# Attention and mixer on one core: the fourth batch's q loaded in token order and turned by DMA transposes

## The chip, the cores and the metric

The kernel runs on one core of one Trainium2 chip. The time is that of the device in microseconds (us), from a whole execution; smaller is better. The profile comes from one execution that the hardware profiler recorded. Its engines are PE (matrix products), PEld (the loading of PE's weights, beside PE), DVE (vector work), ACT (activations), POOL (here mostly the issue of loads that also convert from f32 to f16) and SP (here the issue of stores and of DMA transposes). DMA transfers themselves run on 16 DMA engines.

## What is computed

Attention over a batch of 8, with 8 heads, 576 tokens and 64 columns to a head. Each head has 16 extra keys and values ("beacons") that every token sees; among the 576 tokens the mask is causal. Its output x, 576 tokens by 512 columns to a batch, goes into a mixer: a product of rank 32 along the tokens, then a network of two products with a width of 2048, with both inputs added back.

```python
k_all = np.concatenate([beacon_k, k], axis=2)
v_all = np.concatenate([beacon_v, v], axis=2)
scores = scale * np.matmul(q, k_all.transpose(0, 1, 3, 2))
scores = np.where(causal, -1000000000.0, scores)
a = softmax(scores)                      # written out in the reference
x = np.matmul(a, v_all)                  # heads side by side: (8, 576, 512)
...
h = x.transpose(0, 2, 1) @ U @ V
u = x + h.transpose(0, 2, 1)
out = u + np.maximum(u @ w_ch1, 0.0) @ w_ch2
```

## The kernel before, in words

**Batches and pairs.** The 8 batches are b = 0 to 7; the first is b = 0, so the fourth batch is b = 3. A batch has four pairs of heads, p = 4b to 4b + 3; c = p mod 4 is the pair's place in its batch. The scores of a pair need q and k "turned": 128 rows of head columns (two heads of 64) by tokens. The tiles are qT (one to a batch, two buffers in rotation, for all four pairs) and kTs (two fixed tiles, by b mod 2).

**Two ways to turn.** Up to the fourth batch (b < `DT0` = 4) q and k are loaded by `token_load` so that a partition holds six tokens in a row of each head: 1536 bytes in a piece in memory, 768 bytes once in f16, one load to four heads (`HALVES`). For each pair `regroup` (L290, L292) lets DVE copy the two heads side by side into the tile pr, six identity products on PE turn it (tps, `in_pair`, L297), and one DVE copy moves the 576 columns from PSUM into qT or kT and puts the tokens in order (`qkT_units`, L330; a small one for the beacons of k, L335). From the fifth batch on, `load_whole` loads q and k "whole": five parts of up to 128 tokens, one token to a partition, all eight heads beside one another (L852; a piece is one head of one token, 64 columns, 128 bytes in f16). `turns` then issues five DMA transposes each for q and k from SP (L869); each turns one part for all four pairs.

**Staging.** q and k of a batch land in the tiles st1 and st0, with two buffers each (`qk_tiles`). The buffer of an earlier batch can be loaded again once all its readers are done: regroupings, or DMA transposes.

**Order.** All engines work through instructions in the order in which the program writes them. The loop over pairs p = 8 to 31 does so for the part that matters here. At p = 8 (b = 2, c = 0) `load_batch(3)` issues the loads of the fourth batch on POOL's queue: beacons of k, then k and q by halves of the heads, then v in five parts. At p = 10 `load_whole(4)` appends the loads of the fifth batch, which are issued one with each unit of mixer work. At p = 12 `load_batch(4)` issues v of the fifth batch, `turns(4)` is begun (its first five transposes on SP), then the five transposes uT<-xb of the mixer for b = 2 (`mix_units`, L455), then the other five of `turns(4)`. At p = 13 the loads of b = 5 follow, at p = 15 its transposes.

For p = 8 to 11 the lines in `third` give the order by words: `r` regroups a pair, `q` and `k` turn and evict it, `v` issues scores of pairs and column groups, `m` masks, `a` and `b` are the products with v of the two heads, `f` takes one unit from the queue of mixer work. So "r11 q10 f k10 m8 f v9:123 ..." is p = 8. From p = 12 on `long_slot` gives the order; there the q and k units of pairs 14 and 15 come from the list qk.

**Mixer work between.** The mixer's units are a queue: for each block of 512 rows 16 units g (gps) and then units of the second product (cps in blocks 0 and 1, mps later). Block 0's four stores of ob (L796) and block 1's four transposes ut<-uT (L745), which bring the mixer's input back to rows for the final sum (L790), are issued on SP while pairs 8 to 10 run. For each batch from b = 2 on the five uT<-xb transposes put x into uT, and DVE then adds the rank 32 product to uT in place (`settle`, L476); the next mixer blocks read it.

Of the kernel before, what the change touches and what calls it, by code (L numbers as in the profile page):

```python
# [30 lines left out]
def kernel(  # L31
# [13 lines left out]
    nc = tc.nc  # L45
# [13 lines left out]
    nk = [min(P, SK - P * c) for c in range(NC)]  # L59

    q0 = [max(0, P * j - Nb) for j in range(NC)]
    nq = [min(S, P * (j + 1) - Nb) - q0[j] for j in range(NC)]
    NT = NC
# [42 lines left out]
    def pst(shape, dtype, name):  # L106

        b = emptied.pop(0)
        t = psum.tile(shape, dtype, tag=f"bank{b}", name=name)
        bank_of[id(t)] = (b, t)  # L110
        return t

    def emptying(t):
        emptied.append(bank_of.pop(id(t))[0])
# [62 lines left out]
    kTs = [const.tile([P, NH2, NC * P], F16, name=f"kT{i}", tag=f"kT{i}") for i in range(2)]  # L177
    vss = [const.tile([P, NC * H * E], F16, name=f"vs{i}", tag=f"vs{i}") for i in range(2)]
# [41 lines left out]
    def beacon_load(eng, src, dst, hs):  # L220
        eng.dma_start(out=dst[0:Nb], in_=src[hs].rearrange("h p d -> p h d"))

    def token_load(eng, src, dst, hs):
        eng.dma_start(out=dst[0:TP, hs, :], in_=src[hs].rearrange("h (p j) d -> p h (j d)", j=TJ))  # L224

    def key_beacons(eng, src, dst, hs):
        beacon_load(eng, src, dst[TP:TB, hs, (TJ - 1) * D : TJ * D], hs)
# [4 lines left out]
    def v_beacon(bsrc, vs):  # L232
        beacon_load(nc.gpsimd, bsrc, by_head(vs)[:, 0, :, 0:D], ALLH)

    def v_tokens(src, vs, hs, js=range(NT)):
        dst = by_head(vs)[:, :, hs, 0:D]
        for j in js:
            a = Nb if j == 0 else 0
            nc.gpsimd.dma_start(  # L239
                out=dst[a : a + nq[j], j, :, :], in_=src[hs, ds(q0[j], nq[j]), :].rearrange("h p d -> p h d")  # L240
            )

    def v_loads(src, bsrc, vs):
        v_beacon(bsrc, vs)
        v_tokens(src, vs, ALLH)

    def by_token(t):
        return t.rearrange("p h (j d) -> p j h d", j=TJ)

    ALLH = slice(0, H)  # L250

    def qk_tiles():

        t = [stage.tile([P, TJ * DM], F16, name=f"st{i}", tag=f"st{i}") for i in range(2)]
        st = [x[:, :].rearrange("p (h e) -> p h e", h=H) for x in t]
        whole = [x[:, 0 : NT * DM].rearrange("p (j h d) -> p j h d", h=H, d=D) for x in t]
        return st, whole

    def emit_loads(b, L, vs):
        key_beacons(nc.gpsimd, beacon_k[b], L[0][0], ALLH)  # L260
        for hs in HALVES:
            token_load(nc.gpsimd, k[b], L[0][0], hs)
            token_load(nc.gpsimd, q[b], L[0][1], hs)
        v_loads(v[b], beacon_v[b], vs)


    def keep_warm(ps, n, a=ident):
# [15 lines left out]
    def regroup(st, c, i, *copies, beacons=True):  # L283

        t = pairs.tile([P, TJ, 2, D], F16, name=f"pr{i}", tag=f"pr{i}")
        src = by_token(st[i][:, 2 * c : 2 * c + 2, :])
        w = TJ // len(copies)
        for a, copy in enumerate(copies):
            js = slice(w * a, w * (a + 1))
            copy(out=t[0:TP, js], in_=src[0:TP, js])  # L290
        if i == 0 and beacons:
            copies[0](out=t[TP:TB, TJ - 1], in_=src[TP:TB, TJ - 1])  # L292
        return t
# [15 lines left out]
    def beacons_apart(st, kT, c, copy):  # L309

        ps = pst([P, Nb], F16, name="tpb")
        for h in range(2):
            nc.tensor.transpose(
                ps[ds(D * h, D), :], st[TP:TB, 2 * c + h, ds(D * (TJ - 1), D)], ident[TP:TB, TP:TB]
            )
        copy(out=kT[:, c, 0:Nb], in_=ps)
        emptying(ps)

    def qkT_units(turns, qT, kT, c, copies=((nc.vector.tensor_copy,), (nc.vector.tensor_copy,)), apart=None):

        def one(i, dst, b0):
            w = TJ // len(copies[i])
            bs = 0 if apart else b0
            whole = dst[:, c, b0 : b0 + S].rearrange("x (p j) -> x p j", j=TJ)
            for a, copy in enumerate(copies[i]):
                ps = pst([P, TP * w + bs], F16, name="tps")
                for j in range(w * a, w * a + w):
                    n = TP + bs if j == TJ - 1 else TP
                    turns[i](ps, TP * (j - w * a), n, j)
                copy(  # L330
                    out=whole[:, :, ds(w * a, w)],
                    in_=ps[:, 0 : TP * w].rearrange("x (j p) -> x p j", j=w),
                )
                if bs and a == len(copies[i]) - 1:
                    copies[i][0](out=dst[:, c, 0:b0], in_=ps[:, TP * w : TP * w + b0])  # L335
                emptying(ps)
            if b0 and apart:
                beacons_apart(apart, dst, c, copies[i][0])

        return [lambda: one(1, qT, 0), lambda: one(0, kT, Nb)]  # L340
# [492 lines left out]
    Ls, qTs, xbs = {}, {}, {}  # L833
    coming = []

    def load_batch(b):
        if b < DT0:
            Ls[b] = qk_tiles()
            emit_loads(b, Ls[b], vss[b % 2])
        else:  # L840
            coming.append(lambda: v_beacon(beacon_v[b], vss[b % 2]))
            coming.extend(lambda j=j: v_tokens(v[b], vss[b % 2], ALLH, [j]) for j in range(NT))
# [15 lines left out]
        while coming:  # L858
            coming.pop(0)()

    def turns(b):

        all_coming()
        new_qT(b)
        kn, qn = Ls[b][1]
        k_of = lambda j: (kn, kTs[b % 2], P * j, nk[j], j)
        q_of = lambda j: (qn, qTs[b], q0[j], nq[j], j)
        return [
            lambda n=n, dst=dst, o=o, m=m, j=j: nc.sync.dma_start_transpose(  # L869
                out=dst[:, :, ds(o, m)], in_=n[:m, j, :, :].rearrange("p h d -> p (h d)")  # L870
            )
            for n, dst, o, m, j in [k_of(0), *map(q_of, range(NT)), *map(k_of, range(1, NT))]
        ]

    HALVES = [slice(0, H // 2), slice(H // 2, H)]
# [19 lines left out]
    prs = {}  # L895
    V = nc.vector.tensor_copy

    def regroup_of(p):
        b, c = divmod(p, NH2)
        prs[p] = [regroup(Ls[b][0], c, i, nc.vector.tensor_copy) for i in range(2)]  # L900

    for i in range(2):
        nc.vector.memset(kTs[i][:, :, SK : NC * P], 0.0)
# [15 lines left out]
    def qkT_of(p):  # L919
        b, c = divmod(p, NH2)  # L920
        new_qT_of(p)
        copies = [(act_copy, nc.vector.tensor_copy) if p == 0 else (nc.vector.tensor_copy,)] * 2
        turns = by_heads(Ls[b][0], c)
        for i, t in enumerate(prs.get(p, ())):
            if t is not None:
                turns[i] = in_pair(prs[p])[i]
        return qkT_units(turns, qTs[b], kTs[b % 2], c, copies, Ls[0][0][0] if p == 0 else None)

    def expts_of(p):
        return [(lent if p in (2, 3) else expts)[(2 * p + i) % NE] for i in range(2)]  # L930
# [8 lines left out]
    def av_of(p):  # L939
        b, c = divmod(p, NH2)  # L940
        if c == 0:
            assert not coming or b < DT0
            xbs[b] = xbp.tile([P, NT, DM], F16, name="xb", tag="xb")
# [8 lines left out]
    ON_PE = (0, 1, 4)  # L952

    DT0 = 4
    LAG = 10
    HINT = 5
    FAST = 2
# [10 lines left out]
    def fill_turns(tr, n):  # L968
        for u in tr[:n]:
            u()  # L970
        del tr[:n]
# [25 lines left out]
    def mix(b):  # L997
# [3 lines left out]
        if turned:  # L1001
            turn()
        n = 0 if not turned else LAG + 3 if b == B - 1 else min(LAG, len(queue) - 8)
        k = 2 if turned else 1
# [31 lines left out]
    with tc.manual_schedule(engines={ENG.PE, ENG.Activation, ENG.DVE, ENG.SP, ENG.Pool}):  # L1036
# [15 lines left out]
        for u in qkT_of(1):  # L1052
            u()
# [48 lines left out]
        part = state["part"]  # L1102
# [41 lines left out]

        P6 = (DT0 - 1) * NH2
        mixing = []
# [22 lines left out]
        def long_slot(p, c, av, qk):  # L1169

            if c == 0:
                go([(p + 1, 0), (p + 1, 1), (p + 1, 2)], 1)
                fill(1)
                weighted(av[0:1] + qk[0:1] + av[1:2] + qk[1:2], 1, 1, 0, 1)
                if p + 3 < DT0 * NH2:
                    regroup_of(p + 3)
# [42 lines left out]
        for p in range(NP1, NP):  # L1219
            b, c = divmod(p, NH2)  # L1220
            if c == (1 if b >= DT0 else 0) and b + 1 < B:
                load_batch(b + 1)
            if c == (1 if b + 1 == DT0 else 2) and DT0 <= b + 2 < B:
                load_whole(b + 2)
            qk = qkT_of(p + 2) if P6 <= p and p + 2 < min(NP, DT0 * NH2) else []
            if c == 0 and DT0 <= b + 1 < B and b != DT0:
                tr = turns(b + 1)
            if c == NH2 - 1 and b + 1 == DT0:
                tr = turns(b + 2)
            if c in (0, NH2 - 1) and b + 1 == DT0:  # L1230
                fill_turns(tr, NT)
            if p == P6:
                mix_between(b - 1)
            if c == 0 and b + 1 >= DT0:
                fill_turns(tr, 2 * NT)
            if p < P6:
                play(third[c])
            else:
                long_slot(p, c, av_of(p), qk or [lambda: None] * 2)
# [60 lines left out]
    with tc.If(n_bad != 0, label="general"):  # L1300
        with tc.For_i(0, B, 1) as bi:
            L = qk_tiles()
# [13 lines left out]
            for t0 in range(0, S, 512):  # L1316
                n = min(512, S - t0)
# [32 lines left out]
```

## Time and profile before

| | us |
|---|---|
| median of three timed runs | 343.14 |
| lowest and highest of them | 341.88, 347.04 |
| the profiled execution | 340.93 |
| its span, first to last instruction | 339.3 |
| PE busy in the span | 329.8 |
| DVE busy | 234.1 |
| ACT busy | 178.7 |
| POOL busy | 136.1 |

The granted clock of PE was 1.00 throughout. Rows of a timeline read: start in us from the span's start, duration, engine, line of the kernel, operation, out<-in, shapes and count, and in brackets the idle time before with what ended it; the first start of a row that joins several instructions, and the whole stretch, are given. "SPq" is SP's queue, whose rows are the issue of a DMA, not its transfer. Rows of the DMA view read: what is moved, which queue, how many in the window asked for, KB of each, and last the median time from issue to landing in us. A landing is the point from which a reader may start.

### The profile page before, as it was taken

What the parts mean: (1) busy time and instruction counts of PE and PEld (TensorE: products, weight loads), DVE (VectorE), ACT (ScalarE), POOL (GpSimd) and SP (SyncE); (2) the same over time, 40 slices, a digit from 0 to 9 for tenths busy, and PEclk for the clock granted to TensorE, in tenths of its full rate; (3) what the DMA queues carried; (4) which work ended last, traced back from release to release, by engine and by line L of the source; (5) the groups of instructions that cost most, each with busy time, mean ns of one, the idle gap of its engine ahead of it and who ended that gap; (6) DMA issues with size and microseconds to landing.
All of it is one profiled execution on the core that took longest, in us unless ns stands there. A gap on an engine that the chain in (4) does not pass through costs nothing.

```text
span 339.3 us, 8838 instructions
## 1 busy us (share of the span) xinstructions
PE 329.8 (97%) x3494; PEld 212.0 (62%) x3494; DVE 234.1 (69%) x585; ACT 178.7 (53%) x383; POOL 136.1 (40%) x175
## 2 busy tenths in 40 slices
PE   8799999999999999999999999999999999999993
PEld 4465655455555456865688888755875675585493
DVE  6586885689989748765876677687776963743652
ACT  5957951478851677257734784468445403502500
POOL 8986724765140900677066805040130014013041
PEclk9999999999999999999999999999999999999999
DMA  8999999999997994999999999944213304104113
GB/s 159 141 175 138 183 196 194 200 192 139 138 118 152 153 141 86 101 169 157 151 112 155 187 143 104 132 140 87 66 64 93 73 31 126 31 33 124 31 37 99
DMA packets 150832, 41.97 MB, mean 124 GB/s; under 512 B 132096, under 2 KB 149696, under 8 KB 150784
## 3 DMA queue, kind: packets, MB, share of 16 engines
q0 software_dynamic: 87568, 18.18, 74.6%
q1 hardware_dynamic: 62992, 22.87, 37.4%
q8 instruction: 29, 0.48, 0.6%
q10 hardware_dynamic: 224, 0.30, 0.3%
q14 instruction: 19, 0.16, 0.2%
HBM read 37.45 MB, written 9.44 MB: 138 GB/s over the span
## 4 chain that ended last, share of the span: by engine, by line
PE 88%; DMA 4%; POOL 3%; DVE 1%; issue 1%; ACT 1%; POOLq 0%; DVEq 0%
PE gps L607 29%; PE po L427 9%; PE mpsD L633 7%; PE cps L777 7%; PE gps L751 7%; PE sps L409 5%; DMA vs<-in_v_dram 4%; PE mpsF L633 4%; PE mpsC L633 4%; PE mpsA L633 4%; PE mpsB L633 4%; PE mpsE L633 3%; POOL vs L239 1%; PE sps L370 1%; POOL st L224 1%
## 5 line engine op out<-in xcount | busy, mean ns | idle before, releaser
L418 ACT ACTIVATE expt<-sps 128x496 f16<-128x496 f32 (+2 forms) x192 | 82.0, 539 | 52.6 <-PE sps L409 52.6
L607 PE MATMUL gps<-uT,w 128*128 128x512 f16 (+1 forms) x512 | 103.7, 353 | 0.0
L654 POOL TENSOR_TENSOR ob<-ob,ut 128x512 f32<-128x512 f32 x26 | 30.8, 1188 | 139.9 <-DVE ob L654 127.7
L633 PEld LDWEIGHTS <-gT 128*128 128x128 f16 x800 | 75.1, 98 | 11.3 <-issue 2.1
L618 ACT ACTIVATE gT<-gps 128x512 f16<-128x512 f32 x84 | 49.7, 609 | 58.8 <-PE gps L607 54.3
L607 PEld LDWEIGHTS <-w 128*128 128x128 f16 x512 | 47.6, 98 | 41.4 <-issue 1.6
L239 POOL DMA_DIRECT2D vs<-in_v_dram x50 | 39.7, 804 | 15.3 <-DMA w<-in_moe_w_ch_dram 12.3
L596 DVE TENSOR_TENSOR gT<-gT 128x1024 f16<-128x1024 f16 (+2 forms) x77 | 39.5, 540 | 4.2 <-ACT gT L618 3.3
L427 PEld LDWEIGHTS <-expt 128*128 128x128 f16 x900 | 33.9, 98 | 10.9 <-issue 2.7
L427 PE MATMUL po<-vs,expt 128*128 128x65 f16 x900 | 36.5, 194 | 1.1 <-DMA vs<-in_v_dram 1.0
L616 DVE TENSOR_SCALAR gT<-gps 128x512 f16<-128x512 f32 x28 | 19.3, 691 | 24.0 <-PE gps L607 23.4
L436 DVE TENSOR_TENSOR xb<-po,rec 128x320 f16<-128x320 f32 x64 | 31.4, 491 | 2.2
L751 PE MATMUL gps<-uT,w 128*128 128x512 f16 x128 | 32.5, 379 | 0.1
L777 PE MATMUL cps<-w,gT 128*128 128x512 f16 x128 | 31.1, 379 | 0.0
L435 DVE RECIPROCAL rec<-po 128x5 f32<-128x5 f32 x64 | 12.1, 189 | 19.0 <-PE po L427 18.7
L346 DVE TENSOR_TENSOR expt<-expt,bigmask 128x512 f16<-128x512 f16 x54 | 22.5, 417 | 1.2 <-ACT expt L418 1.2
L409 PE MATMUL sps<-qT,kT 64*128 64x80 f16 (+4 forms) x288 | 22.6, 281 | 0.0
L376 ACT ACTIVATE expt<-sps 128x496 f16<-128x496 f32 (+2 forms) x48 | 20.4, 564 | 0.6 <-PE sps L370 0.6
L409 PEld LDWEIGHTS <-kT 64*128 64x128 f16 x288 | 10.2, 94 | 13.4 <-issue 9.3
L777 PEld LDWEIGHTS <-gT 128*128 128x128 f16 x128 | 11.2, 98 | 11.6 <-issue 1.3
L852 POOL DMA_DIRECT2D st<-in_q_dram x20 | 16.9, 874 | 3.2 <-DVE expt L348 1.4
L751 PEld LDWEIGHTS <-w 128*128 128x128 f16 x128 | 10.6, 97 | 10.8 <-issue 1.2
(125 smaller groups left out, 384.8 us busy)
## 6 DMA issues: line engine op xcount, KB each, us to landing
out_dram<-ob SPq DMA_DIRECT2D x55, 128.0 KB, 1.9
vs<-in_v_dram POOLq DMA_DIRECT2D x18, 128.0 KB, 7.9
w<-in_moe_w_ch_dram POOLq DMA_DIRECT2D x4, 512.0 KB, 6.4
w<-in_moe_w_ch_dram POOLq DMA_DIRECT2D x2, 1024.0 KB, 12.8
out_dram<-ob SPq DMA_DIRECT2D x8, 256.0 KB, 4.9
st<-in_k_dram POOLq DMA_DIRECT2D x12, 128.0 KB, 7.2
st<-in_q_dram POOLq DMA_DIRECT2D x12, 128.0 KB, 8.3
st<-in_k_dram POOLq DMA_DIRECT2D x4, 288.0 KB, 11.9
```

Source lines behind the costliest of these rows:

```text
L239: nc.gpsimd.dma_start(out=dst[a : a + nq[j], j, :, :], in_=src[hs, ds(q0[j], nq[j]), :].rearrange("h p d -> p h d"))
L409: nc.tensor.matmul(banks[i][:, ds(at0 + o, w)], kT[hp, c, ds(P * ch, P)], qT[hp, c, ds(qa, w)], start=True, stop=True, skip_group_check=le ...
L418: nc.scalar.activation(out=at[p][3][i][:, ds(SLOT * g, gw[g])], in_=bank[:, ds(at0, gw[g])], func=AF.Exp, scale=scale)
L427: nc.tensor.matmul(po[:, j, :], ex[0 : nk[c], ds(blk[(c, j)], P)], vs[0 : nk[c], ds(c * H * E + h * E, E)], start=(c == 0), stop=(c == j),)
L436: nc.vector.tensor_tensor(out=xb[:, :, ds(h * D, D)], in0=po[:, :, 0:D], in1=r.broadcast_to([P, NT, D]), op=ALU.mult)
L596: nc.vector.tensor_tensor(out=o[:, ds(d0, n)], in0=x[:, ds(d0, n)], in1=y[:, ds(d0, n)], op=op)
L607: nc.tensor.matmul(g[:, ds(o, w)], w1[:, cc, ts(dc, P)], uT[:, cc, ds(at, w)], start=(cc == 0 and o == 0), stop=(cc == NCC - 1), skip_grou ...
L618: nc.scalar.activation(out=cell["g"][:, dc, :], in_=g, func=AF.Relu)
L633: nc.tensor.matmul(ps, a()[:, d, ds(P * i, P)], bm[:, d, ds(c0, w)], start=fresh and d == 0 and (i == 0 or key != bank), stop=d == HF - 1, ...
L654: eng.tensor_tensor(out=out, in0=x, in1=y, op=ALU.add)
L751: nc.tensor.matmul(g[:, 0:n], w1[:, cc, ts(dc, P)], uT[:, cc, ds(r0, n)], start=(cc == 0), stop=(cc == NCC - 1))
L777: nc.tensor.matmul(ps[:m, :], gT["t"][:, dc, ds(P * i, m)], w2[:, dc, :], start=(dc == 0), stop=turned and dc == NDC - 1, skip_group_check ...
```

## The change

A new constant `AHEAD = "q"` names what the fourth batch loads whole. `load_batch(3)` then issues on POOL: beacons of k, the two halves of k, five parts of q in token order, and v as before. Right behind it, still at the top of p = 8, the five DMA transposes of q are issued on SP into qT of that batch. For the pairs 12 to 15 the regrouping of q, its six identity products and its eviction are left out; an empty unit stands where they stood. k of that batch is loaded, regrouped and turned as before.

```diff
-    def emit_loads(b, L, vs):
-        key_beacons(nc.gpsimd, beacon_k[b], L[0][0], ALLH)
+    def emit_loads(b, L, vs, whole=""):
+        if "k" not in whole:
+            key_beacons(nc.gpsimd, beacon_k[b], L[0][0], ALLH)
         for hs in HALVES:
-            token_load(nc.gpsimd, k[b], L[0][0], hs)
-            token_load(nc.gpsimd, q[b], L[0][1], hs)
+            for i, (name, src) in enumerate((("k", k[b]), ("q", q[b]))):
+                if name not in whole:
+                    token_load(nc.gpsimd, src, L[0][i], hs)
+        if whole:
+            for u in whole_loads(b, L, whole):
+                u()
         v_loads(v[b], beacon_v[b], vs)
+
+    def whole_loads(b, L, names):
+
+        def part(i, j):
+            src, m = ((k[b], nk), (q[b], nq))[i]
+            nc.gpsimd.dma_start(
+                out=L[1][i][m[j] - nq[j] : m[j], j, :, :],
+                in_=src[:, ds(q0[j], nq[j]), :].rearrange("h p d -> p h d"),
+            )
+
+        units = []
+        if "k" in names:
+            units += [lambda: beacon_load(nc.gpsimd, beacon_k[b], L[1][0][:, 0, :, :], ALLH)]
+        units += [lambda n=n, j=j: part("kq".index(n), j) for n, j in order_of(names)]
+        return units
+
+    def order_of(names):
+
+        return [x for x in [("k", 0)] + [("q", j) for j in range(NT)] + [("k", j) for j in range(1, NT)] if x[0] in names]
...
-            emit_loads(b, Ls[b], vss[b % 2])
+            emit_loads(b, Ls[b], vss[b % 2], AHEAD if b == DT0 - 1 else "")
...
-    def turns(b):
+    def turns(b, names="kq"):
...
-            for n, dst, o, m, j in [k_of(0), *map(q_of, range(NT)), *map(k_of, range(1, NT))]
+            for n, dst, o, m, j in [(k_of if x == "k" else q_of)(i) for x, i in order_of(names)]
...
-        prs[p] = [regroup(Ls[b][0], c, i, nc.vector.tensor_copy) for i in range(2)]
+        prs[p] = [
+            None if b == DT0 - 1 and name in AHEAD else regroup(Ls[b][0], c, i, nc.vector.tensor_copy)
+            for i, name in enumerate("kq")
+        ]
...
-        return qkT_units(turns, qTs[b], kTs[b % 2], c, copies, Ls[0][0][0] if p == 0 else None)
+        units = qkT_units(turns, qTs[b], kTs[b % 2], c, copies, Ls[0][0][0] if p == 0 else None)
+        return [
+            (lambda: None) if b == DT0 - 1 and name in AHEAD else u for name, u in zip("qk", units)
+        ]
...
+    AHEAD = "q"
...
             if c == (1 if b >= DT0 else 0) and b + 1 < B:
                 load_batch(b + 1)
+                if b + 1 == DT0 - 1:
+                    fill_turns(turns(b + 1, AHEAD), 2 * NT)
```

## The prediction

> **What bounds the kernel now.** I read the page first: its span and its chain of work.
>
> ```profile
> span 339.3 us, 8838 instructions
> PE 88%; DMA 4%; POOL 3%; DVE 1%; issue 1%; ACT 1%; POOLq 0%; DVEq 0%
> ```
>
> PE holds 88% of the chain, so time is won by taking work from PE and lost by making PE wait. Next I read the stretches in which q and k of the fourth batch (b = 3, head pairs p = 12 to 15) are turned. The columns are the busy time of PE, PEld, DVE, ACT and POOL, the granted clock, the DMA share and GB/s.
>
> ```profile
> 72.00:80.00 8.00, 7.48 (x103) 4.48 (x101) 7.55 (x20) 6.12 (x14) 5.51 (x7) 1.00 2.48 148
> 96.00:104.00 8.00, 8.00 (x77) 4.10 (x74) 7.58 (x20) 2.43 (x6) 0.75 (x2) 1.00 2.04 159
> ```
>
> PE is full but for 0.52 us, at full clock; DVE has under half a microsecond to spare in eight; and DMA's share is above 2, packets queueing on one another. So here three things are nearly full at once. What is removed loads PE and DVE; what is added loads DMA and the two queues that issue it, POOL's and SP's.
>
> **What is removed.** The timeline of PE, with the first and the last of the four groups of q transposes (six in a group, one group to a pair):
>
> ```profile
> 81.77 0.42 PE L297 MATMUL tps<-ident,pr 96*128 96x96 f16 x6
> 82.03 1.03 PE L751 MATMUL gps<-uT,w 128*128 128x512 f16 x4
> ...
> 85.03 0.69 PE L409 MATMUL sps<-qT,kT 64*128 64x336 f16 x10
> ...
> 101.60 0.42 PE L297 MATMUL tps<-ident,pr 96*128 96x96 f16 x6
> 101.86 1.03 PE L777 MATMUL cps<-w,gT 128*128 128x512 f16 x4
> ...
> 110.08 0.76 PE L409 MATMUL sps<-qT,kT 64*128 64x208 f16 x8
> ```
>
> The next matmuls start 0.26 us after a group does (82.03 - 81.77, 101.86 - 101.60). Four groups give PE 4 x 0.26 = 1.04 us, and PE is the path: a gain of 1.0 us if nothing else comes late. DVE's timeline:
>
> ```profile
> 99.91 0.36 DVE L290 COPY pr<-st 96x768 f16<-96x768 f16 x1
> 100.19 0.68 DVE L790 TENSOR_TENSOR ob<-cps,ut 128x512 f32<-128x512 f32 x1
> ...
> 102.28 0.75 DVE L330 COPY qT<-tps 128x576 f16<-128x576 f16 x1
> ...
> 104.87 2.42 DVE L476 TENSOR_TENSOR uT<-ups,uT 128x496 f16<-128x496 f32 x4
> ...
> 108.43 0.75 DVE L330 COPY kT<-tps 128x576 f16<-128x576 f16 x1
> 109.10 0.16 DVE L335 COPY kT<-tps 128x16 f16<-128x16 f16 x1
> ```
>
> DVE loses four regroupings and four evictions of q, 4 x (0.36 + 0.75) = 4.4 us. That is worth what PE waits for DVE there: between 0 and the 0.52 us above. I take 0, since that one wait falls before the first of the evictions.
>
> **What is added on the load queue.** POOL's timeline, and for the same instructions (in the same order, the two last for the loads at 78.31 and 83.53) the microseconds from issue to landing, last column of the DMA view:
>
> ```profile
> 61.51 0.67 POOL L224 DMA_DIRECT2D st<-in_k_dram  x1
> 62.32 0.67 POOL L224 DMA_DIRECT2D st<-in_q_dram  x1
> 63.62 0.54 POOL L221 DMA_DIRECT2D vs<-in_beacon_v_dram  x1 [0.63 <-PE cps L785]
> ...
> 69.63 0.73 POOL L239 DMA_DIRECT2D vs<-in_v_dram  x1 [1.09 <-PE cps L785]
> ...
> 78.31 0.82 POOL L852 DMA_DIRECT2D st<-in_q_dram  x1 [1.42 <-DVE expt L348]
> ...
> 83.53 0.74 POOL L852 DMA_DIRECT2D st<-in_q_dram  x1 [1.37 <-DMA st<-in_k_dram]
> ...
> 109.62 0.54 POOL L221 DMA_DIRECT2D st<-in_beacon_k_dram  x1 [12.87 <-DMA kT<-st]
> ```
>
> ```profile
> st<-in_k_dram POOLq DMA_DIRECT2D x1, 288.0 KB, 9.2
> ...
> st<-in_q_dram POOLq DMA_DIRECT2D x1, 288.0 KB, 10.1
> ...
> vs<-in_beacon_v_dram POOLq DMA_DIRECT2D x1, 16.0 KB, 9.3
> ...
> vs<-in_v_dram POOLq DMA_DIRECT2D x1, 80.0 KB, 9.6
> ...
> st<-in_q_dram POOLq DMA_DIRECT2D x1, 112.0 KB, 8.8
> ...
> st<-in_q_dram POOLq DMA_DIRECT2D x1, 80.0 KB, 6.3
> ```
>
> The second half of k lands at 61.51 + 9.2 = 70.7, the second half of q at 72.4: a half of q takes the queue 1.7 us, both 3.4. The whole form isn't in the trace for this batch, but v's five parts have its shape: 72.9 (63.62 + 9.3) to 79.2 (69.63 + 9.6), 6.3 us, or 1.26 a part. So everything behind q in this queue is 6.3 - 3.4 = 2.9 us later: v of this batch, and k and q of the fifth. The first half of q no longer precedes k's second half, which lands at 70.7 - 1.7 = 69.0; q's parts follow at 70.3, 71.5, 72.8, 74.0 and 75.3.
>
> **What is added on SP.** SP's timeline, and landings of the transposes that it issues:
>
> ```profile
> 70.43 6.09 SPq L745 DMA_TRANSPOSE ut<-uT  x4
> 85.42 1.19 SPq L869 DMA_TRANSPOSE kT<-st  x1
> 87.15 5.31 SPq L869 DMA_TRANSPOSE qT<-st  x4
> 92.55 7.64 SPq L455 DMA_TRANSPOSE uT<-xb  x5
> ...
> 101.53 6.29 SPq L869 DMA_TRANSPOSE kT<-st  x4
> ```
>
> ```profile
> ut<-uT SPq DMA_TRANSPOSE x4, 8.6
> ...
> uT<-xb SPq DMA_TRANSPOSE x1, 5.5
> ...
> ut<-uT SPq DMA_TRANSPOSE x4, 2.3
> ```
>
> The first landing row is for the four at 70.43, the second for the fourth of the five from 92.55 (issued at 97.63 in a narrower window), the third for four late ones at 285, when no loads run. The five new transposes stand in SP's program behind the third store of block 0 and ahead of its fourth store, of the four ut transposes and of all that follows. They wait for q's parts, so SP issues them from 70.3 to 76.6 (75.3 plus 1.3 for one). Queued behind them are that store, which nobody reads, and ut, now from 76.6 to 82.7, landed by 91.3 with 8.6; its first reader is the DVE row at 100.19. Both are covered.
>
> Landing is 8.6 us as for the ut at the same place: the fourth at 74.0 + 8.6 = 82.6, the fifth at 83.9. PE's first scores of this batch start at 85.03 - 0.26 = 84.8 and need the first four. Covered by 2.2 us.
>
> The Trainium skill, DMA: Bandwidth & Descriptors, section "Queues, rings and completion order", says that each DMA engine goes round robin between the queues that have work, a packet at a time. By that the transposes would not stand behind loads already queued, and the sum would be that of the first rival, a gain. The rows 8.6 with loads queued and 2.3 without do not bear it out in full.
>
> **The hidden wait.** The beacon load at 109.62 starts batch b = 5's k and waited 12.87 us, for the last kT transposes of b = 4 (issued until 101.53 + 6.29 = 107.8). So it was given the staging buffer of b = 4, whose readers came earlier in the program than the last regrouping of b = 3: buffers are handed on in the order in which their last reader is written. In the changed program q's staging buffer of b = 3 has its last reader, the five transposes, ahead of r11, the last reader of b = 2's. So b = 4's q should get b = 3's buffer, and its loads must wait for the fifth landing, 83.9, instead of starting at 78.31. I start them at 84.3 and give the first 6.3 us, the load nearest in time (8.8 is the other end): 90.6, against 78.31 + 8.8 = 87.1. SP's qT transposes of b = 4, which took up their work at 87.15 when that part had landed, start at 90.6, **3.5 us later**, and SP runs without a pause from there through the five uT<-xb. The fourth of these lands at 97.63 + 5.5 + 3.5 = 106.6 instead of 103.1.
>
> On it waits the DVE row at 104.87, which adds the mixer's product to uT in place: 1.7 us late. DVE works in order, and behind it stands the eviction of the last k (108.43, ending with its beacons at 109.26), now done by 111.0. PE would reach the scores at 110.08 by 110.08 - 1.02 = 109.06 (all four groups gone) and waits for that k until 111.0. So the sum at this place is 111.0 - 110.08 = **+0.9 us**: the gain of 1.0 and a stall of 1.9. After it SP's lead over PE is 2.6 us smaller (3.5 - 0.9), which later pauses of SP take up.
>
> **The sum.** The profiled execution took 340.93 us with its span of 339.3; that gives 341.8. The three timed runs have their median at 343.14 and reach from 341.88 to 347.04, so on their scale the forecast is 343.1 + 0.9 = **344.0**. Within 2% (6.9 us) is about what a measurement of this kernel tells from no change.
>
> **The rivals.**
> 1. No stall. If b = 4's q gets b = 2's buffer after all, its loads are later by the queue's 2.9 us at most, and by nothing if the transposes land sooner than 8.6. uT's fourth then lands at 103.1 to 106.0. From the DVE row at 104.87 to the end of k's eviction it is 4.39 us, so PE, there at 109.06, notices nothing up to 104.67: the whole 1.0 us is left, 342.1. At 106.0 it would be +0.3. For it: landings of 2.3 to 5.5 us where fewer loads were queued. Against it: the 12.87 us wait.
> 2. Slower. The same chain with the longest landing of this stretch at both steps. The load of q at 62.32 took 10.1: the fifth transpose then lands at 75.3 + 10.1 = 85.4, the first q load of b = 4 at 85.8 + 10.1 = 95.9, SP is 8.8 us late, uT's fourth lands at 111.9, the last k is evicted at 109.26 + 7.0 = 116.3: +6.2 us, and with the queue's own 2.9 us on top of the second landing +9.1. Middle, 343.1 + 7.6 = 350.7. It decides from an uT landing at 112.6 on, where the loss passes 6.9. For it: the DMA share of 2.0 to 2.5 from 72 to 104, to which five transposes are added. Against: the loads' own landings were down from 10.1 to 6.3 by 83.53, before the place where the second long one is needed.
> 3. PE waits for q itself, at the scores of 85.03. It does if the new transposes take over 10.8 us to land (8.6 + 2.2). At 3.2 us later than I have it PE stands 1.0 us there, and the same lateness goes on through the buffer to uT: its fourth lands at 109.8, the last k is evicted at 114.2, +4.1 us, 347.2.
>
> That PE's q work doesn't go at all isn't possible: no q group is left for these four pairs.
>
> **How the numbers follow.** Forecast 0.45, its own range 342.5 to 346.5; rival 1 0.27; rival 2 0.20, of which one case in six stays within 2%; rival 3 0.08. Faster by over 2% would need 6.9 us where PE's q work is 1.0: 0.03, taken from rival 1 for what no row here shows. Slower by over 2%: 0.19, from rival 2 and a tail of rival 3. Within 2%: 0.78. The range must keep rival 1 (342.1, less the 1.3 us by which the lowest run lies under the median) and most of rival 2: 341.0 to 350.5.
>
> **What would show it.** The PE groups of q for pairs 12 to 15 gone; five qT transposes on SP between 70 and 77 and landed by 84; q loads of b = 4 starting at about 84 with a wait put down to a qT landing; uT<-xb starting at about 96 instead of 92.55; a PE idle of about 2 us ahead of the scores at 110, released by the eviction of kT. If the loads of b = 4's q start at 78 to 81, the hidden wait is wrong and rival 1 holds. If uT<-xb starts after 102, rival 2 does. What would make all of it wrong is a wait of POOL or SP for something that neither queue waited for before, such as a transpose that is held until loads ahead of it have landed.

## Result, and the profile after

| | before | after |
|---|---|---|
| median, 21 runs each (us) | 343.42 | 346.61 |
| lowest and highest (us) | 339.80, 349.91 | 344.29, 349.11 |
| the profiled execution, its span (us) | 340.93, 339.3 | 348.38, 346.7 |
| mean granted clock in it | 1.000 | 0.988 |

The ratio after to before is **1.0146, with a 95% interval of 1.0116 to 1.0177**: some 5 us slower. That ratio leaves out runs more than 1.5% above the fastest of their kernel, which are ten of before's 21 (346.69 to 349.91, as long as after's) and none of after's, so it sets all of after's runs against before's shorter half; over all runs the medians are 3.2 us apart and the means 1.9. The two profiles below are of a short execution of before and a long one of after, 7.45 us apart. The forecast was 344.0 with a range from 341.0 to 350.5 and a loss within 2%.

The page of the kernel after: its span, busy times, granted clock in 40 slices, and the chain of work.

```profile
span 346.7 us, 8793 instructions
...
PE 332.7 (96%) x3470; PEld 212.1 (61%) x3470; DVE 228.3 (66%) x577; ACT 178.5 (51%) x383; POOL 138.1 (40%) x178
...
PEclk9999999999999699999999999999999999999998
...
PE 86%; DMA 4%; ACT 3%; DVE 3%; SPq 2%; issue 1%; DVEq 0%
```

PE has 24 instructions fewer (3494 before) and DVE 8 fewer (585), as the change intends. Yet PE is busy 2.9 us longer than before's 329.8. The clock row says why: one slice, from 113 to 121 us, has a 6. What precedes it stands in PE's timeline, first before, then after:

```profile
106.11 0.43 PE L297 MATMUL tps<-ident,pr 96*128 96x96 f16 x6
...
107.39 2.75 PE L777 MATMUL cps<-w,gT 128*128 128x512 f16 x12
...
110.76 2.76 PE L777 MATMUL cps<-w,gT 128*128 128x512 f16 x12
```

```profile
105.02 0.43 PE L321 MATMUL tps<-ident,pr 96*128 96x96 f16 x6
...
106.29 1.89 PE L801 MATMUL cps<-w,gT 128*128 128x512 f16 x8
110.29 1.02 PE L801 MATMUL cps<-w,gT 128*128 128x512 f16 x4 [2.11 <-DVE uT L500]
111.25 0.45 PE L433 MATMUL sps<-qT,kT 64*128 64x208 f16 x2
113.93 1.16 PE L433 MATMUL sps<-qT,kT 64*128 64x208 f16 x6 [2.23 <-DVE kT L354]
115.02 5.02 PE L801 MATMUL cps<-w,gT 128*128 128x512 f16 x12
```

At the last group of k PE is 1.1 us ahead of before (105.02 against 106.11; 0.3 of it was there at 63, where the first of the changed loads had only just been issued: 63.21 against 63.51). Then it waits twice, 2.11 and 2.23 us, each time for a DVE row. After that the same twelve products take 5.02 us instead of 2.76. They end at 120.04, where before has 113.52: **6.5 us late**, and 6.5 it stays until PE's last product. The other 0.9 of the 7.4 us between the spans lies behind that, in the last eviction and store.

The stretches of the kernel after (columns: busy time of PE, PEld, DVE, ACT and POOL, granted clock, DMA share, GB/s) show the clock:

```profile
108.00:110.00 2.00, 0.18 (x1) 0.00 (x0) 0.43 (x1) 0.00 (x0) 0.00 (x0) 1.00 0.65 48
...
112.00:114.00 2.00, 0.07 (x2) 0.07 (x3) 1.97 (x6) 0.00 (x0) 0.00 (x0) 0.70 0.38 77
114.00:116.00 2.00, 2.00 (x9) 0.67 (x10) 2.00 (x4) 1.62 (x6) 0.40 (x1) 0.50 0.68 228
116.00:118.00 2.00, 2.00 (x7) 0.63 (x5) 1.63 (x6) 1.28 (x3) 2.00 (x4) 0.50 0.82 212
118.00:120.00 2.00, 2.00 (x7) 0.79 (x6) 0.00 (x0) 0.00 (x0) 2.00 (x3) 0.59 1.43 91
```

Half clock from about 112.8 for 6.8 us (1.2 us of the stretch with 0.70, four whole, 1.6 of the one with 0.59). DVE does no more than 0.43 us from 108 to 110, so it wasn't slow but stood for something. The chain in order of time names it:

```profile
103.90 5.54 DMA uT<-xb
...
109.56 2.42 DVE uT L500 x4
...
113.20 0.68 DVE kT L354
...
113.93 1.16 PE sps L433 x6
```

The fourth uT<-xb lands at 109.44 instead of 103.12. DVE adds into uT at 109.56 instead of 104.87, so the eviction of the last k, behind it in DVE's order, ends at 113.94 instead of 109.26. That is the path that the prediction had drawn, with a lateness of 6.3 us instead of 3.5. SP's timeline, and then POOL's, show where it was gathered:

```profile
71.42 8.11 SPq L893 DMA_TRANSPOSE qT<-st  x5
...
80.44 6.84 SPq L769 DMA_TRANSPOSE ut<-uT  x4
87.46 1.67 SPq L893 DMA_TRANSPOSE kT<-st  x1
92.66 6.62 SPq L893 DMA_TRANSPOSE qT<-st  x4
99.37 7.46 SPq L479 DMA_TRANSPOSE uT<-xb  x5
```

```profile
75.73 4.19 POOL L876 DMA_DIRECT2D st<-in_k_dram  x5
80.85 2.59 POOL L876 DMA_DIRECT2D st<-in_q_dram  x3 [0.93 <-DVE expt L372]
83.73 0.88 POOL L876 DMA_DIRECT2D st<-in_q_dram  x1 [0.30 <-DMA st<-in_k_dram]
85.06 0.73 POOL L876 DMA_DIRECT2D st<-in_q_dram  x1 [0.45 <-DMA st<-in_k_dram]
```

The loads of b = 4's q start at 80.85, before the fifth of the new transposes has landed (85.56): they did not wait for it. But the first took longer. In the DMA view of the kernel after (last column: median us to landing) it reads so, and below it the new transposes:

```profile
st<-in_q_dram POOLq DMA_DIRECT2D x1, 112.0 KB, 11.8
```

```profile
qT<-st SPq DMA_TRANSPOSE x5, 7.8
```

So that part lands at 92.6 (before: 87.1), and SP, which stands from 89.13 for it, is 5.5 us late at the qT of b = 4 and 6.8 late at uT<-xb.

### The profile page after: what moved, and what is told of

Its sections match the earlier page's. It is cut to its first block, busy times and chain, and to the rows that moved or that the text cites. A ratio compares the mean times of both kernels' runs of the same rounds, so it can differ in the third digit from the quotient of the medians.

```text
span 346.7 us, 8793 instructions
## 1 busy us (share of the span) xinstructions
PE 332.7 (96%) x3470; PEld 212.1 (61%) x3470; DVE 228.3 (66%) x577; ACT 178.5 (51%) x383; POOL 138.1 (40%) x178
## 4 chain that ended last, share of the span: by engine, by line
PE 86%; DMA 4%; ACT 3%; DVE 3%; SPq 2%; issue 1%; DVEq 0%
PE gps L631 28%; PE po L451 8%; PE mpsD L657 7%; PE cps L801 7%; PE gps L775 6%; PE sps L433 5%; PE mpsF L657 4%; PE mpsC L657 4%; PE mpsB L657 4%; PE mpsA L657 4%; PE mpsE L657 3%; ACT expt L400 2%; DMA qT<-st 2%; DMA uT<-xb 2%; PE idle L296 1%; SPq L893 1%
## 5 line engine op out<-in xcount | busy, mean ns | idle before, releaser
L801 PE MATMUL cps<-w,gT 128*128 128x512 f16 x128 | 33.2, 400 | 2.1 <-DVE uT L500 2.1
L433 PE MATMUL sps<-qT,kT 64*128 64x80 f16 (+4 forms) x288 | 23.6, 285 | 3.1 <-DVE kT L354 2.2
L500 DVE TENSOR_TENSOR uT<-ups,uT 128x496 f16<-128x496 f32 x24 | 14.5, 664 | 6.2 <-DMA uT<-xb 5.7
```

Source lines behind the costliest of these rows:

```text
L433: nc.tensor.matmul(banks[i][:, ds(at0 + o, w)], kT[hp, c, ds(P * ch, P)], qT[hp, c, ds(qa, w)], start=True, stop=True, skip_group_check=le ...
L801: nc.tensor.matmul(ps[:m, :], gT["t"][:, dc, ds(P * i, m)], w2[:, dc, :], start=(dc == 0), stop=turned and dc == NDC - 1, skip_group_check ...
```

## The experiments

Two places matter: **A**, the scores at 110, and **B**, the same step one batch later, at 145. At B the five uT<-xb transposes of b = 3 stand on SP behind the first transposes of b = 5, and the fourth of them holds a DVE row (L476, L500 after) on which PE's next PSUM bank (mpsE) waits. The first four runs were made on one chip, with 342.0 us (339.94 to 344.95, 7 runs) for the kernel before.

**Order on SP (a_ut_first).** The kernel after, but at p = 12 the uT<-xb transposes ahead of the first five for b = 4:

```diff
-            if c in (0, NH2 - 1) and b + 1 == DT0:
-                fill_turns(tr, NT)
             if p == P6:
                 mix_between(b - 1)
+            if c in (0, NH2 - 1) and b + 1 == DT0:
+                fill_turns(tr, NT)
```

> The changed kernel with one swap in SP's order at p = 12: the five uT<-xb transposes stand ahead of the first five transposes of the fifth batch, not behind them. Theory (SP order): in the changed kernel uT lands late (109.4 us) only because SP stood at 87 to 92.7 waiting for the fifth batch's q ahead of it. Then uT<-xb is issued from about 92 and has landed by 104, DVE does not wait for it, PE has no idle at 106 to 114, the clock stays at 1.00, and the time is that of before less the 1.0 us of PE's q groups plus up to 0.9 us of the wait at 85: ratio to before 0.996 to 1.000. Rival (DMA volume): the DMA engines are so full from 70 to 104 that uT lands late wherever it stands in SP's order: landing after 107, ratio 1.008 to 1.015.

348.84 us (346.02 to 350.56), ratio 1.0191 (1.0100 to 1.0281). Waits of this kernel from 80 to 160 us (total, times, longest), and then two rows of its PE timeline:

```profile
DVE uT L500 <- DMA uT<-xb: 7.0, 2, 4.8
```

```profile
145.53 1.03 PE L657 MATMUL mpsE<-wt,gT 128*128 128x256 f16 x8 [1.70 <-DVE uT L500]
...
147.27 0.37 PE L433 MATMUL sps<-qT,kT 64*128 64x496 f16 x1 [0.25 <-DVE uT L500]
```

The uT<-xb start at 91.60, but with b = 4's loads in flight the fourth lands only at 105.53; PE waits 1.16 us at A, and from 1.5 ahead of before it comes to level. Then it loses 3.9 us at B, where the order was left as it was. Neither reading foresaw that: undoing the order at A alone leaves 1.16 us of the wait there and moves the loss to B.

**Loads alone (b_whole_on_pe).** The kernel after without the five new transposes; PE turns q's whole rows by five identity products a pair:

```diff
-            (lambda: None) if b == DT0 - 1 and name in AHEAD else u for name, u in zip("qk", units)
+            (lambda: q_direct(b, c)) if b == DT0 - 1 and name in AHEAD else u for name, u in zip("qk", units)
...
+    def q_direct(b, c):
+        ps = pst([P, S], F16, name="tps")
+        for j in range(NT):
+            n = nq[j]
+            nc.tensor.transpose(ps[:, ds(q0[j], n)], Ls[b][1][1][:n, j, 2 * c : 2 * c + 2, :], ident[:n, :n])
+        nc.vector.tensor_copy(out=qTs[b][:, c, 0:S], in_=ps)
+        emptying(ps)
...
-                if b + 1 == DT0 - 1:
-                    fill_turns(turns(b + 1, AHEAD), 2 * NT)
```

> The loads alone: q of the fourth batch is loaded whole as in the changed kernel, but no DMA transpose turns it; PE turns it by five identity products a pair straight from the loaded tile, and DVE evicts it as before (no regrouping). If the five added transposes make the lateness (through SP's order and by their share of the DMA engines), the fifth batch's q lands about 88 to 89, uT at 104 to 105 and the ratio to before is 0.997 to 1.003. If the longer loads make it, q of the fifth batch lands after 91, uT after 107, and the ratio is 1.008 or more.

347.11 us (346.42 to 347.96), ratio 1.0122 (1.0035 to 1.0210). There is no wait at A: the fourth uT<-xb lands at 104.24, within the 104 to 105 expected. The ratio came out above the range that went with it, because at B there is a wait, in its PE timeline, and in the view of stretches the clock from 146 to 154 is 0.57:

```profile
145.08 1.03 PE L657 MATMUL mpsE<-wt,gT 128*128 128x256 f16 x8 [2.19 <-DVE uT L500]
...
150.60 3.45 PE L657 MATMUL mpsD<-w,gT 128*128 128x256 f16 x16
```

```profile
146.00:154.00 8.00, 7.63 (x35) 3.98 (x34) 5.48 (x12) 3.08 (x8) 3.54 (x4) 0.57 1.14 147
```

PE goes from 0.9 ahead of before to 5.9 behind. What tips it shows in SP's and POOL's timelines of this kernel, then in the same two of before, then for the fourth uT<-xb in this kernel's DMA view, and last in the DMA view of before:

```profile
135.05 6.41 SPq L479 DMA_TRANSPOSE uT<-xb  x5
...
138.19 4.23 POOL L239 DMA_DIRECT2D vs<-in_v_dram  x5
```

```profile
131.19 7.03 SPq L455 DMA_TRANSPOSE uT<-xb  x5
...
139.12 4.23 POOL L239 DMA_DIRECT2D vs<-in_v_dram  x5
```

```profile
uT<-xb SPq DMA_TRANSPOSE x1, 5.3
```

```profile
uT<-xb SPq DMA_TRANSPOSE x1, 2.5
```

The fourth is issued from 138.90, just behind the first v load of b = 5 (138.19), and takes 5.3 us; before, it was issued from 135.66, ahead of v's loads (139.12), and took 2.5. SP is 3.9 us later here than before (135.05 against 131.19), and 3.2 at that issue becomes 6.1 at the landing (144.23 against 138.15). The other two kernels that lose at B show the same: in a_ut_first the fourth is issued at 139.90, 0.8 us behind the first of v's loads (139.13), and takes 4.7; in c_extra_turns, below, at 141.96, 0.1 us ahead of it (142.07), and takes 5.3.

**Transposes alone (c_extra_turns).** The kernel before, with five extra DMA transposes at the same place of SP's program, from q's staging buffer of b = 3, 96 rows each instead of up to 128, into a part of wt that is unused then (`spare`); nobody reads their output, so this adds their time and one more reader of that buffer.

```diff
...
+                if b + 1 == DT0 - 1:
+                    for j in range(NT):
+                        nc.sync.dma_start_transpose(
+                            out=spare[:, :, ds(TP * j, TP)],
+                            in_=Ls[b + 1][1][1][:TP, j, :, :].rearrange("p h d -> p (h d)"),
+                        )
```

> The transposes alone: the kernel before with five more DMA transposes on SP at the place where the change has its own; they turn q of the fourth batch (96 rows each instead of up to 128) into a part of a tile that is not yet in use, and nobody reads what they write. All else is as before, PE's q groups too. If the transposes make the lateness: q of the fifth batch lands after 90, uT at 106 to 109, PE idles before the scores at 110, ratio 1.004 to 1.014. If they do not, 0.999 to 1.003.

349.35 us (346.03 to 350.71), ratio 1.0162 (1.0057 to 1.0267), above the range expected, since B is lost as well as A. Its SP timeline, and then its PE timeline:

```profile
68.10 6.77 SPq L1226 DMA_TRANSPOSE wt<-st  x5
...
93.48 5.72 SPq L869 DMA_TRANSPOSE qT<-st  x4
99.30 7.24 SPq L455 DMA_TRANSPOSE uT<-xb  x5
```

```profile
111.28 0.82 PE L409 MATMUL sps<-qT,kT 64*128 64x208 f16 x6 [1.70 <-DVE kT L330]
...
148.19 1.03 PE L633 MATMUL mpsE<-wt,gT 128*128 128x256 f16 x8 [1.42 <-DVE uT L476]
```

SP is 6.3 us late at qT of b = 4 with before's own loads, so the five transposes by themselves make the lateness. They make it through the landing of the first of b = 4's q loads, for which SP waits. The DMA view of the loads alone, and then of the transposes alone:

```profile
st<-in_q_dram POOLq DMA_DIRECT2D x1, 112.0 KB, 6.7
```

```profile
st<-in_q_dram POOLq DMA_DIRECT2D x1, 112.0 KB, 13.3
```

Before it was 8.8. The starts of that load differ by less: 78.31 before, 82.19 with the loads alone, 80.14 with the transposes alone, 80.85 after. Both A and B are lost, with the clock at half for 3.4 us behind the first and 6.8 behind the second. Next to each other, A reads:

| | SP at qT of b = 4 | uT<-xb starts | the fourth lands | PE goes on with the scores |
|---|---|---|---|---|
| before | 87.15 | 92.55 | 103.12 | 110.08, no wait |
| loads alone | 88.92 | 96.20 | 104.24 | 109.15, no wait |
| transposes alone | 93.48 | 99.30 | 106.79 | 111.28 |
| after | 92.66 | 99.37 | 109.44 | 113.93 |

In the two that wait PE goes on 4.49 us after the landing; a_ut_first does the same (105.53 and 110.03). So the rest of the chain adds nothing of its own there: the landing decides.

**The clock (d_warm).** The kernel after, with twelve idle products put into a PSUM bank ahead of the uend products of b = 2, so that PE is busier ahead of its waits.

```diff
+            if u0 == 2 * S:
+                bank = pst([P, 512], F32, name="uend")
+                keep_warm(bank, 12)
+                ups = bank[:, 0 : NCC * n].rearrange("p (c n) -> p c n", n=n)
...
```

> The changed kernel with 12 idle matmuls on PE (512 columns each, about 2.6 us at full clock) ahead of the uend products of b = 2, in the bank that these overwrite. uT still lands at 109 and the scores still wait for k's eviction, but PE's idle time falls from 4.3 us to about 2. Theory: the clock at 0.50 for 6.8 us follows from PE's idle time and costs 3.3 us; it stays at 1.00 and the ratio to before falls from 1.0146 to about 1.005. Rival: the clock falls all the same, or the stall grows by what is filled in: ratio 1.014 to 1.020.

349.16 us (348.33 to 350.83), ratio 1.0199 (1.0108 to 1.0291). Of its PE timeline, the filling and the two waits:

```profile
105.80 2.32 PE L296 MATMUL uend<-ident 128*128 128x512 f16 x10
...
111.22 1.02 PE L806 MATMUL cps<-w,gT 128*128 128x512 f16 x4 [1.22 <-DVE uT L500]
...
114.86 0.82 PE L433 MATMUL sps<-qT,kT 64*128 64x208 f16 x6 [2.23 <-DVE kT L354]
```

The two waits came to 3.45 us instead of 4.34, not the 2 expected, and half clock lasted 3.4 us instead of 6.8. But PE is 6.5 us behind before all the same: in this run the fourth uT<-xb landed at 110.37 instead of 109.44, and PE went on with the scores 0.93 us later. The expected gain didn't come, neither here nor in the median; the ratio is the one that the rival had. How much of half clock the filling saves by itself isn't settled by it; it doesn't touch what makes PE wait.

**The right order, with and without the change (f to i).** Four kernels on one chip with 343.07 us (339.64 to 350.75, 31 runs) for before. In each the same two lines are removed, so that the first five transposes of the next batch no longer stand ahead of uT<-xb, neither at p = 12 nor at p = 15 (A and B); they follow with the other five.

```diff
-            if c in (0, NH2 - 1) and b + 1 == DT0:
-                fill_turns(tr, NT)
```

f_after_late is the kernel after with this, g_before_late the kernel before, h_on_pe_late the loads alone, and i_kq_late the kernel after with `AHEAD = "kq"`, so that k of b = 3 goes by DMA transposes too.

> The changed kernel without the early five transposes of the next batch, at p = 12 and at p = 15: all ten of a batch now stand on SP behind the five uT<-xb. Theory (one cause, two places): the added work makes SP late against PE, and the loss comes where uT<-xb then lands after DVE wants it, at 105 (b = 2) or at 140 (b = 3), in each execution at one of the two; PE's wait halves the clock for 3.4 to 6.8 us. With uT<-xb first at both places there is at most the 1 us at 110 that the swap alone still showed (DMA engines full, landing 105.5), no wait at 145, clock 1.00: ratio to before 0.999 to 1.005. Rival: the DMA engines are simply too full for the added transposes, and the loss moves on to a third place: ratio 1.010 or more.

> The kernel before with the same removal of the early five. Theory: the kernel before stands 1.5 to 2 us from the same edge at 140 (landing 138.15 for a use at 139.94); its slower executions, which show a clock under 0.996, are those that fall over it. With uT<-xb first they go: all executions within 1% of one another, median 340 to 342, ratio to the fast runs of before 0.994 to 1.000. Rival: its slower executions have another cause: they stay, ratio 1.000 with the same spread.

> The loads alone (q of the fourth batch whole, turned by five identity products a pair on PE) without the early five. The loads-alone kernel lost all of its 6.9 us at 145 and was 0.6 us ahead of before until then. Theory: that loss goes, ratio 0.996 to 1.000, executions within 1%. Rival (full DMA engines): 1.008 or more.

> Both q and k of the fourth batch whole and turned by ten DMA transposes at p = 8, without the early five later. PE loses another 1.0 us of k groups, DVE 4 us; the loads take 3 us more and five more transposes go into the full stretch at 70 to 90. If SP's order was all, the ratio is 0.995 to 1.003. If the DMA engines are the limit, PE waits at 85 for q and k by 3 to 8 us and the ratio is 1.010 to 1.030.

| | median (us) | lowest, highest | ratio to before |
|---|---|---|---|
| f: after, order changed | 341.08 | 340.13, 342.82 | 0.9979 (0.9939 to 1.0019) |
| g: before, order changed | 340.46 | 339.65, 341.41 | 0.9941 (0.9902 to 0.9980) |
| h: loads alone, order changed | 341.50 | 339.53, 343.93 | 0.9951 (0.9904 to 0.9999) |
| i: q and k, order changed | 343.82 | 341.88, 347.73 | 1.0042 (0.9981 to 1.0103) |

With that order the loss of the change is gone. The expectations held in the main: f and h lie a little below their ranges, h's executions spread by 1.3% instead of 1%, and i's ratio lies just above 1.003. The SP timeline of f, and then its PE timeline:

```profile
72.18 8.09 SPq L893 DMA_TRANSPOSE qT<-st  x5
...
80.99 8.38 SPq L769 DMA_TRANSPOSE ut<-uT  x4
93.36 7.73 SPq L479 DMA_TRANSPOSE uT<-xb  x5
```

```profile
86.43 0.39 PE L433 MATMUL sps<-qT,kT 64*128 64x496 f16 x2 [1.10 <-DMA qT<-st]
```

The same 8 us of new transposes stand on SP, and still uT<-xb starts at 93.36, since nothing ahead of it waits for b = 4's q. Neither A nor B shows a wait of PE above 0.3 us. A is passed narrowly, though: the fourth uT<-xb lands at 106.11, and DVE waits 1.0 us for it. What is left is a wait of 1.10 us for q itself at 86, which is as much as PE's q work: f is 0.6 us above g in the medians of ten runs each. So without the disturbance the change gains nothing, and **the best version is g**, which does without it: it is below both kernels. Its highest run is 341.41, where before, on the same chip, reached 350.75 with the same lowest time. The place B explains that well (before's fourth uT<-xb lands at 138.15 and v's loads start at 139.12, a margin of 1 us; in g it lands at 136.09). The mean clocks fit it too: 0.987 to 0.994 in the twelve of before's executions that took 344.7 us or more, 0.996 or more in all ten of g. But there is no trace of one of before's long executions, so it is argued and not shown. In h, the profiled run had half clock at 16 us, far ahead of the change; what caused that stays open. In i PE waits 2.7 us in all for the k transposes at 87 to 90, and its fourth uT<-xb lands at 107.72: with ten transposes more, PE waits for the data itself.

## Why the prediction was right or wrong

The sign, the place A and the chain from uT's landing to PE were right, and the time lies in the range. Three steps failed (2, 3 and 7 below), one term was mis-sized (4) and one was missing (6). That SP's lateness at b = 4's q came out near the forecast is luck: a wait that does not exist stood in for a landing that was taken too short.

| step | predicted | measured |
|---|---|---|
| parts of q land | 70.3 to 75.3 | 71.4 to 75.4 |
| five new transposes issued | 70.3 to 76.6 | 71.4 to 79.5 |
| fourth and fifth land | 82.6, 83.9 | 84.9, 85.6 |
| PE at the scores of b = 3 | covered by 2.2 | waits 0.86 |
| q loads of b = 4 start | 84.3 | 80.85 |
| the first of them takes | 6.3 | 11.8 |
| SP at qT of b = 4 | 90.6 | 92.7 |
| uT<-xb starts, the fourth lands | 96, 106.6 | 99.4, 109.4 |
| last k evicted | 111.0 | 113.9 |
| granted clock | 1.00 | 0.50 for 6.8 us |

1. **What is removed: right, a little low.** Four groups are 1.04 us, and the 0.52 us of PE's wait from 72 to 80, which I had taken as not won, went too. PE's lead grew from 0.31 us (75.35 against 75.66) to 1.07 (79.23 against 80.30) before any group was gone; with the first group it was 1.3 at 84. That this was DVE's relief is not shown: with the transposes alone, where DVE does all the work on q, the wait is gone as well (79.54 against 80.30).
2. **The covered step at 84.8: wrong.** The five transposes' issue took 8.1 us where 6.3 was taken (one alone 2.6), so the fourth landed at 84.9, 2.3 later than taken. PE was 0.6 us earlier there than I had it (85.05 - 0.86 = 84.2), so it waited 0.86 us. The row at 85.03 was misread as well: of its ten scores the first eight don't wait for this q (in the kernel after they run at 83.71), so PE needs it some 0.5 us later than I took. This is rival 3 in small. I had tied that rival to a landing of over 10.8 us, and landings were 6.5 to 8.3: the delay came through the issue instead, where one of the five took 2.63 us and the others 1.2 to 1.3.
3. **The hidden wait: wrong.** The loads started at 80.85; my own sign for this failure was a start from 78 to 81. The inference from one long wait of POOL (12.87 us) to which buffer is handed to whom did not hold for this pair.
4. **The landing of those loads: mis-sized.** I took 6.3 us and kept 8.8 as the other end; it was 11.8. This error and the one before cancel in part: 84.3 + 6.3 = 90.6 against 80.85 + 11.8 = 92.6. The same load took 6.7 us with the loads alone and 13.3 with the transposes alone. SP got to qT at 88.9 with the loads alone and at 93.5 with the transposes alone, so it is mainly the transposes in that stretch that make b = 4's q late.
5. **The chain from there: right.** With the measured landing the prediction's arithmetic gives DVE's row at 109.56, thus 4.69 late, and the last k at 109.26 + 4.69 = 113.95; measured 113.94. Instead of +0.9, PE's scores are then 113.93 - 110.08 = 3.85 us late.
6. **The clock: missing.** The sum had nothing for it. The twelve cps took 5.02 - 2.76 = 2.26 us more; the six scores took 1.16, where eight had taken 0.76 before, 0.40 more. 3.85 + 2.26 + 0.40 = 6.5, the whole lateness in the profiled run.
7. **"Later pauses of SP take up" the lost lead: wrong.** Loads alone passed A without a wait and lost at B. SP's lateness is handed on: b = 5's loads wait for b = 4's k transposes (they start at 112.17 there, at 109.62 before), its qT transposes wait for those loads (124.59 against 120.80), and uT<-xb stands behind them (135.05 against 131.19).

Rival 1 (no stall) falls with the chain at A, though its reason, no hidden wait, was true. Rival 2 is nearest in mechanism, but only at its second step: the first q load of b = 4 took 11.8 us where it had 10.1, while the new transposes' own landings, 6.5 to 8.3, were no longer than the forecast's 8.6. Its price was 7.6 us without the clock; measured were 3.85 with 2.66 more from the clock.

## What to carry to other kernels

Before putting DMA transposes on an in-order queue, list what stands behind them there, and find the one that the next loads' landing will hold: its lateness, not the engine time saved, is the price. Ask of the kernel before how far its own hot transfer is from the first load behind which it would land late; here that was 1 us, and putting the hot transposes first gained 2.6 us in the medians, more than the change's 1.0 us of PE work. A wait of 2 us on PE is to be priced with what the clock may take on top, here up to 2.7 us.

## What the runs showed of the hardware that was not expected

- **Short waits were followed by half clock.** With nothing else above 0.3 us near them, a wait of 2.19 us (loads alone, at B) was followed by 6.8 us at 0.50, one of 1.42 us (transposes alone, at B) likewise, and one of 1.70 at A by 3.4 us. But 1.70 us in a_ut_first at B was followed by none, so the length of one wait doesn't decide. In the clock records of the ten traces every stretch at one clock but the last, such as 105.81 us at full clock and then 6.83 at half in the kernel after, is a multiple of 3.413 us (31 and 2 of them). In the 3.41 us just ahead of half clock PE stood, all pauses together, for 2.01 us in the kernel after, 1.81 in the loads alone, 1.70 (A) and 1.67 (B) in the transposes alone, 2.23 in d_warm and 2.11 in i_kq_late; a_ut_first had 1.70 in such a stretch without it. So as long as PE has work, the sum within one such stretch, about half of it, is nearer to what decides than one wait's length; where the edge lies isn't measured, and h's half clock at 16 came after only 1.00. The Trainium skill, TensorE: Matmul & The Clock Gate, section "HAM oscillation — how this bites in real kernels", gives the rule that idle gaps of PE should stay below some 3.4 us. The lengths 3.4 and 6.8 agree with one and two windows of the size which that page gives; the rule itself differs, since here waits well below it cost clock, and the measurement decides.
- **A transpose's landing depends sharply on loads around it.** The same uT<-xb took 2.5 us ahead of v's loads and 5.3 just behind the first of them; in the stretch from 71 to 80, with loads all around, the new ones took 7.8. The Trainium skill, DMA: Bandwidth & Descriptors, section "Queues, rings and completion order", has each engine take turns between queues by packets; that alone would not lead one to expect such a step.
- **The issue of a transpose on SP isn't constant.** Of the five new ones in the stretch from 71 to 80 four took 1.2 to 1.3 us and one 2.63. That isn't the traffic alone: before has one of 2.32 at 104.20, where DMA's share was below 1. What holds single ones stays open.
